# One tile shape for neighbouring matmuls in an attention and two-MLP kernel

## The chip, the cores and the metric

The kernel runs on one core of a Trainium2 chip. The metric is the device time of one execution in microseconds (us). Five engines work side by side and wait for each other through semaphores: TensorE (PE, with its weight loads listed as PEld), VectorE (DVE), ScalarE (ACT), GpSimd (POOL) and SyncE (SP), which issues the DMAs.

## The reference

The inputs are q, k, v of shape (4, 8, 576, 64) and a gate f of shape (4, 8, 576). In the computation below S = 576 and D = 64.

```python
scores = np.matmul(q, k.transpose(0, 1, 3, 2)) / np.sqrt(D)
cum = np.cumsum(np.log(np.clip(f, 0.0001, 1.0)), axis=-1)
decay = cum[:, :, :, None] - cum[:, :, None, :]
scores = np.where(causal, -1e9, scores + decay)      # causal: keys after the query
attn = np.exp(scores - scores.max(-1, keepdims=True))
attn = attn / (attn.sum(-1, keepdims=True) + 1e-9)
x = (attn @ v)                                       # then (2304 tokens, 512)
h = x @ w_in;   x = where(h >= 1, h, where(h <= -1, 0, (h + 1)**2 / 4)) @ w_out
h = x @ w_in2;  out = (P(h) / (Q(h) + 1e-6)) @ w_out2
```

P is a cubic in h with the four coefficients a, Q is 1 + |b0||h| + |b1|h². The weights are 512 x 2048 and 2048 x 512 and come as 64-bit floats.

## The kernel before

**Attention.** The 32 heads go in 16 pairs; the two heads of a pair lie in the lower and upper 64 partitions. For a pair, `tasks_of_pair` makes tasks for 9 blocks of queries. The first block holds the last 64 queries of both heads against all 576 keys (128-row matmuls, line 405). The other eight are four blocks of 128 queries for each of the two heads, against 512, 384, 256 and 128 keys. One task, S, computes such a block for both heads (line 414): four steps, each two matmuls side by side, one for each head in its own 64 partitions. The first three steps are the split products of q and k (each in a high and a low part, to keep fp32 accuracy): ql with kh, qh with kl, qh with kh. The fourth adds the decay of the keys: `one`, all ones, by `c_`, whose rows 0 and 1 (64 and 65 for the second head) hold the high and low part of the cumulated log of f; its other rows are zero. That step uses only 2 rows. M (VectorE) adds the causal mask and takes the maximum, E (ACT) the exp with its sum, T (line 460) transposes the block's exps in chunks of 128 keys into PSUM, C copies them to SBUF, and V (line 500) multiplies with v, chunk by chunk, for two groups of queries (256 and 320 wide), the two heads in two halves of the output's partitions. The fifth chunk has only 64 keys: its transpose has 64 columns, its product 64 rows. R1 to R6 divide: reciprocals of nine sums for each query (VectorE), a transpose of those 9 columns (line 528), a copy, a trip through memory that spreads them over partitions, and a product on POOL; X stores the pair's result.

**Filling work and MLPs.** During the attention, parts of the first MLP for early tokens fill the TensorE's free time (lines 683 and 764), and the 64-bit weights are turned into fp32 by steps on ACT and VectorE and split by ACT and POOL. Behind the attention both MLPs run over the rest (lines 683, 777, 779).

**The order.** It is written by `plan`, a list scheduler: each task has an engine, a duration, what it needs, and a key for its place; at each turn the task that can start first (with a small addition for its key) is taken, and buffers and queues are kept by the same durations. `plan` runs once for the attention with its filling work and once for the rest. Each engine then works off its own tasks in that order. So the durations given to S (line 424) and V (line 507) also set the order of all other tasks.

Of the kernel before, what the change touches and what calls it, by code (L numbers as in the profile page):

```python
# [7 lines left out]
F32 = mybir.dt.float32  # L8
# [4 lines left out]
ALU = mybir.AluOpType  # L13
# [5 lines left out]
def kernel(ctx, tc, qT, kT, v, f, w_in1, w_out1, w_in2, w_out2, a, b, out):  # L19
# [9 lines left out]
    P = 128  # L29
# [20 lines left out]
    CS = 12.0  # L50
    WARM, WARM2 = 12, 14
    WK = 0.003

    const = ctx.enter_context(tc.tile_pool(name="const", bufs=1))
    dram = ctx.enter_context(tc.tile_pool(name="dram", bufs=1, space=DRAM))
# [124 lines left out]
    kt, qt = [[[ap1.tile([P, S], F32R, name=f"{x}{y}{n}") for y in "hl"] for n in range(2)] for x in "kq"]  # L180
    qd = [[ap1.tile([P, P], F32R, name=f"qd{y}{n}") for y in "hl"] for n in range(2)]
    ct = [ap1.tile([P, S], F32R, name=f"ct{n}") for n in range(2)]
    one, oned = [ap1.tile([P, P], F32R, name=f"one{x}") for x in range(2)]
    half = ap1.tile([P, 2], F32, name="half")
    POOL.memset(half[:], 0.0)
# [16 lines left out]
    def load_pair(pr, x):  # L202
        if x < 2:
            t = ap2.tile([P, S], F32, tag=("ks", "qs")[x], name=f"{'kq'[x]}s{pr}")
            SP.dma_start(t[:], (kT, qT)[x][pr])
        else:
            t = ap2.tile([P, NC, P], F32, tag="vn", name=f"vn{pr}")
            SP.dma_start(
                t[:, 0:NC - 1, :], v[pr, 0:(NC - 1) * P, :].rearrange("(c p) d -> p c d", p=P)
            )  # L210
            SP.dma_start(t[0:QB, NC - 1, :], v[pr, (NC - 1) * P:S, :])
        nat[pr, x] = t

    def load_c(pr):
# [20 lines left out]
    def task(key, eng, dur, fn, deps=(), take=(), free=()):  # L235
# [2 lines left out]
        tasks.append((key, ways, tuple(d for d in deps if d is not None), tuple(take), tuple(free)))  # L238
        return len(tasks) - 1

    done, by = {}, {}
    clock = dict.fromkeys(LAT, T0)
    clock["sp"] = 3.0
    dma = [3.0, 5.0]
# [3 lines left out]
    def plan(first, wk):  # L248
        left, users = {}, {}
        for n in range(first, len(tasks)):  # L250
            users.setdefault(n, [])
            left[n] = 0
            for d in tasks[n][2]:
                if d >= first:
                    users.setdefault(d, []).append(n)
                    left[n] += 1
        ready = {n for n, k in left.items() if k == 0}
        order = []
        while ready:
            best = None  # L260
            for n in ready:
                key, ways, deps, take, _ = tasks[n]
                free_at = 0.0
                ok = True
                need = {}
                for tag in take:
                    k = need[tag] = need.get(tag, 0) + 1
                    if len(bufs[tag]) < k:
                        ok = False
                        break  # L270
                    free_at = max(free_at, sorted(bufs[tag])[k - 1])
                if not ok:
                    continue
                choice = None
                for w, (eng, dur, _) in enumerate(ways):
                    at = max(clock[eng], free_at)
                    for d in deps:
                        e2 = by[d]
                        at = max(at, done[d] + (0.13 if e2 == eng and eng != "pe" else 0.0 if e2 == eng else LAT[e2]))
                    end = at + dur if len(ways) > 1 else 0.0  # L280
                    if choice is None or end < choice[0]:
                        choice = (end, at, w)

                cand = (choice[1] + wk * key, key, n, choice[1], choice[2])
                if best is None or cand < best:
                    best = cand
            assert best, [(tasks[n][0], tasks[n][3]) for n in ready]
            _, key, n, at, w = best
            _, ways, _, take, free = tasks[n]
            eng, dur, fn = ways[w]  # L290
            ready.discard(n)
            by[n] = eng
            for tag in take:
                bufs[tag].remove(min(bufs[tag]))
            if eng == "sp":
                for issue, moved in dur:
                    dma[0] = max(dma[0], at) + issue
                    dma[1] = max(dma[1], dma[0] + 0.64) + MOVE * moved
                clock[eng] = dma[0]
                done[n] = dma[1] + LAND  # L300
            elif eng == "init":
                done[n] = dur
            else:
                clock[eng] = at + dur
                done[n] = at + dur
            for tag in free:
                bufs[tag].append(done[n] + LAT[eng])
            order.append((at, n, fn))
            for u in users[n]:
                left[u] -= 1  # L310
                if left[u] == 0:
                    ready.add(u)
        assert len(order) == len(left), (len(order), len(left))
        order.sort(key=lambda t: t[:2])
        return [t[1:] for t in order]

    def mm(n, passes=1):
        return passes * (max(n, 64) / 2400 + 0.013)
# [20 lines left out]
    def tasks_of_pair(pr):  # L339
# [48 lines left out]
        for pos, (b, j) in enumerate(BLOCKS):  # L388
# [8 lines left out]
            def s_fn(s=s, b=b, both=both, cuts=cuts):  # L397
# [12 lines left out]
                qc = slice(b * P, (b + 1) * P)  # L410
                for x, (qq, kk_) in enumerate(((ql_, kh), (qh, kl_), (qh, kh), (one, c_))):
                    for jj in range(2):
                        pp = slice(jj * QB, jj * QB + (QB if x < 3 else 2))
                        PE.matmul(  # L414
                            ts[jj][:, 0:n], qq[pp, qc] if x < 3 else qq[pp, :], kk_[pp, 0:n], start=(x == 0), stop=(x == 3)
                        )
# [3 lines left out]
            if j == 1:  # L420
                tid[pr, f"S{pos}"] = tid[pr, f"S{pos - 1}"]
            else:
                dur = 4 * sum(mm(n1 - n0) for n0, n1 in cuts) if both else 4 * max(mm(w), 0.22)
                T(f"S{pos}", s, "pe", 0.08 + dur, s_fn, ("klo", "ldc", "qlo", "qd0", "qd1", prev), ("S", "S"),
                  ("k", "q") if pos == NB - 2 else ())

            def max_fn(s=s, w=w, pos=pos, both=both):
                if pos == 0:
# [22 lines left out]

            firstg = pos == min(p for p, (bb_, _) in enumerate(BLOCKS) if int(bb_ * P >= GQ[0]) == g)
            for c0, c1 in [(0, LAST), (LAST, NC)] if both else [(0, b + 1)]:
                rows = QB if c0 == LAST else P

                def t_fn(s=s, c0=c0, c1=c1, rows=rows):
                    p = Pt[s]
                    ps = Tt[s, c0] = psT.tile([P, 512], F32, tag="T", name=f"T{s}_{c0}")
                    for c in range(c0, c1):
                        PE.transpose(  # L460
                            ps[0:rows, (c - c0) * P:(c - c0 + 1) * P], p[:, c * P:c * P + rows], ident[:]
                        )

                T(f"T{pos}_{c0}", s + KT, "pe", 0.107 * (c1 - c0), t_fn, (f"E{pos}",),
                  ("T",), ("P",) if c1 == b + 1 else ())

                def c_fn(eng, s=s, g=g, j=j, qo=qo, c0=c0, c1=c1, rows=rows, both=both):
                    if (pr, g) not in PT:
                        PT[pr, g] = ap1.tile([P, 2 + 3 * g, 2, GQ[g]], F32, tag=f"PT{g}", name=f"PT{pr}_{g}")
                    to, src = PT[pr, g], Tt.pop((s, c0))  # L470
                    n = (c1 - c0) * P
                    if both:
                        copy(eng, to[0:rows, c0:c1, :, qo:qo + QB], src[0:rows, 0:n].rearrange("p (c j x) -> p c j x", j=2, x=QB))
                    else:
                        copy(eng, to[0:rows, c0:c1, j, qo:qo + P], src[0:rows, 0:n].rearrange("p (c x) -> p c x", x=P))

                engs = ["act", "dve"]
                T(f"C{pos}_{c0}", s + KC, engs, [cost(e, (c1 - c0) * P, "ps") for e in engs],
# [5 lines left out]
        for g in (1, 0):  # L484
# [4 lines left out]
            deps = [k for k in list(tid) if k[0] == pr and k[1][0] == "C" and int(k[1][1:].split("_")[0]) in poss]  # L489
            for c in range(ncs):  # L490
                c_q = max(0, c * P - q0)
                rows = QB if c == LAST else P

                def pv_fn(g=g, c=c, c_q=c_q, rows=rows, n=n, ncs=ncs):
                    if c == 0:
                        Ot[pr, g] = psO.tile([P, 512], F32, tag="O", name=f"O{pr}_{g}")
                    o, pt = Ot[pr, g], PT[pr, g]
                    for j in range(2):
                        pp = slice(j * D, (j + 1) * D)
                        PE.matmul(  # L500
                            o[pp, c_q:n], nat[pr, 2][0:rows, c, pp], pt[0:rows, c, j, c_q:n],
                            start=(c == 0), stop=(c == ncs - 1),
                        )
                    if c == ncs - 1:
                        PT.pop((pr, g))

                T(f"V{g}{c}", s0 + last + KV, "pe", mm(n - c_q, 4) + 0.06, pv_fn,
                  deps + ["ldv"] + ([f"V{g}{c - 1}"] if c else []) + (["V14"] if g == 0 else []), ("O",) if c == 0 else (),
                  ((f"PT{g}",) + (("v",) if g == 0 else ())) if c == ncs - 1 else ())

            def o_fn(eng, g=g, q0=q0, n=n):
                if g == 1:
# [6 lines left out]


        def r1():
            r = Rt[pr] = ap2.tile([P, NB], F32, tag="r", name=f"r{pr}")
            DVE.tensor_scalar(out=r[:], in0=ls[pr][:], scalar1=1e-9, scalar2=None, op0=ALU.add)
            DVE.reciprocal(r[:], r[:])

        def r2():
            Rr[pr] = psT.tile([P, 512], F32, tag="T", name=f"rT{pr}")
            PE.transpose(Rr[pr][0:NB, 0:P], Rt[pr][:], ident[:])  # L528

        def r3():  # L530
            ps = Rr[pr]
# [560 lines left out]
```

## Time and profile before

| | |
|---|---|
| median of 3 runs | 1021.68 us (1020.82 to 1025.32) |
| the profiled execution | 1021.83 us, span 1020.0 us |
| mean granted TensorE clock | 0.990 |
| TensorE busy | 1003.8 us (98%), 5274 matmuls |
| weight loads busy | 796.4 us (78%) |
| VectorE busy | 739.6 us (73%) |
| ScalarE busy | 631.9 us (62%) |
| GpSimd busy | 377.0 us (37%) |

The span is the time from the first to the last instruction. TensorE's matmuls are pipelined and overlap in the trace, so that "busy" says little of how full it is; the distance from one start to the next is of more use. A line such as "64\*128 64x512" gives the rows and columns of the weights and the shape of the streamed operand. In the trace "L414" is line 414 of the kernel before.

### The profile page before, as it was taken

The page shows a single profiled execution, that of the slowest core. Times are in us where ns is not written, and L with a number is a line of the kernel's source. Part 1 is how long each engine was busy: PE and PEld are TensorE (multiplying, and loading weights), DVE is VectorE, ACT ScalarE, POOL GpSimd, SP SyncE. Part 2 cuts the span into 40 slices and gives each one's busy share as a digit, 9 for nine tenths or more (in the row PEclk, how much of TensorE's full clock was granted, in tenths as well). Part 3 has the DMA queues.
Part 4 walks back from the last instruction along what each step waited for, and adds up shares of the span by engine and source line. Part 5 has one row for each costly group of instructions (what it writes and reads, how often), then busy time and mean ns, then how long its engine had stood idle before and what let it go on. Part 6 is the DMA issues. An engine that isn't in the chain of part 4 may idle for free.

```text
span 1020.0 us, 15449 instructions
## 1 busy us (share of the span) xinstructions
PE 1003.8 (98%) x5274; PEld 796.4 (78%) x5274; DVE 739.6 (73%) x1411; ACT 631.9 (62%) x1312; POOL 377.0 (37%) x331
## 2 busy tenths in 40 slices
PE   8999999999999999999999999999999999999998
PEld 4665666666767888888888998888888888888887
DVE  6888997867287798786874577967667667657646
ACT  5787777767455443433432468876677667666666
POOL 3223320122365532222222133545454444445344
PEclk7999999999999999999999999999999999999999
DMA  5455766622456347565561454001101000010010
GB/s 187 152 176 172 220 204 204 190 67 69 158 189 227 118 152 238 161 205 166 156 225 63 131 179 125 1 10 33 42 0 42 8 35 16 6 42 1 1 42 21
DMA packets 62790, 113.13 MB, mean 111 GB/s; under 512 B 9452, under 2 KB 20348, under 8 KB 62712
## 3 DMA queue, kind: packets, MB, share of 16 engines
q1 hardware_dynamic: 62712, 112.15, 34.5%
q8 instruction: 42, 0.69, 0.3%
q14 instruction: 36, 0.29, 0.1%
HBM read 82.00 MB, written 30.11 MB: 110 GB/s over the span
## 4 chain that ended last, share of the span: by engine, by line
PE 89%; DVE 4%; ACT 2%; issue 2%; DMA 1%; POOL 1%; SPq 1%; ACTq 0%; DVEq 0%
PE h L683 35%; PE a L779 18%; PE a L777 16%; PE S L414 6%; PE T L460 5%; PE O L500 5%; PE a L764 2%; PE S L405 1%; DVE xl L672 1%; POOL wl L130 1%; ACT P L448 0%; DMA xr<-xd 0%; ACT PT L329 0%; DMA qs<-in_q_dram 0%; PE rT L528 0%
## 5 line engine op out<-in xcount | busy, mean ns | idle before, releaser
L697 POOL TENSOR_TENSOR gl<-t,gh 128x512 fp32r<-128x512 f32 (+1 forms) x160 | 195.7, 1224 | 323.3 <-ACT gh L693 238.9
L683 PE MATMUL h<-xl,wh 128*128 128x512 f32 (+1 forms) x640 | 236.5, 370 | 2.4 <-DVE xl L672 2.1
L683 PE MATMUL h<-xh,wl 128*128 128x512 f32 (+1 forms) x640 | 237.2, 371 | 1.0 <-ACT xh L668 1.0
L683 PE MATMUL h<-xh,wh 128*128 128x512 f32 (+1 forms) x640 | 235.6, 368 | 0.0
L693 ACT CAST gh<-t 128x512 fp32r<-128x512 f32 (+1 forms) x160 | 93.0, 582 | 112.7 <-PE a L779 47.8
L728 POOL TENSOR_TENSOR t<-t,t 128x512 f32<-128x512 f32 (+1 forms) x80 | 94.5, 1181 | 126.8 <-ACT t L721 123.4
L683 PEld LDWEIGHTS h<-xl,wh 128*128 128x128 f32 x640 | 120.7, 189 | 25.1 <-DVE xl L672 5.8
L683 PEld LDWEIGHTS h<-xh,wl 128*128 128x128 f32 x640 | 120.7, 189 | 22.3 <-ACT xh L668 1.4
L683 PEld LDWEIGHTS h<-xh,wh 128*128 128x128 f32 x640 | 120.7, 189 | 19.9
L779 PE MATMUL a<-wh,gl 128*128 128x512 f32 x288 | 112.3, 390 | 0.0
L779 PE MATMUL a<-wl,gh 128*128 128x512 f32 x288 | 112.2, 390 | 0.0
L779 PE MATMUL a<-wh,gh 128*128 128x512 f32 x288 | 112.1, 389 | 0.0
L777 PE MATMUL a<-gl,wh 128*128 128x512 f32 (+1 forms) x288 | 105.3, 366 | 0.0
L777 PE MATMUL a<-gh,wl 128*128 128x512 f32 (+1 forms) x288 | 105.3, 366 | 0.0
L777 PE MATMUL a<-gh,wh 128*128 128x512 f32 (+1 forms) x288 | 105.3, 365 | 0.0
L707 ACT ACTIVATE t<-t 128x512 f32<-128x512 f32 (+1 forms) x80 | 47.1, 589 | 91.6 <-DVE t L702 91.3
L746 DVE SCALAR_TENSOR_TENSOR t<-t,na,h 128x512 f32<-128x512 f32 (+1 forms) x80 | 55.4, 692 | 57.2 <-ACT h L742 56.1
L448 ACT ACTIVATE P<-P,nm 128x576 f32<-128x576 f32 (+2 forms) x144 | 83.7, 584 | 19.1 <-DVE nm L436 16.9
L702 DVE TENSOR_SCALAR t<-h 128x512 f32<-128x512 f32 (+1 forms) x80 | 50.7, 633 | 58.5 <-PE h L683 58.4
L732 DVE TENSOR_TENSOR t<-h,t 128x512 f32<-128x512 f32 (+1 forms) x80 | 51.0, 637 | 48.8 <-ACT t L724 48.5
L436 DVE CUSTOM_DVE_ANT_0 P<-S,tri 128x256 f32<-128x256 f32 (+1 forms) x144 | 66.9, 477 | 17.1 <-PE S L414 15.8
L718 ACT ACTIVATE t<-h,ab 128x512 f32<-128x512 f32 (+1 forms) x80 | 51.9, 651 | 41.9 <-PE h L683 41.7
(115 smaller groups left out, 1905.5 us busy)
## 6 DMA issues: line engine op xcount, KB each, us to landing
raw<-in_moe_w_in_dram SPq DMA_DIRECT2D x32, 512.0 KB
raw<-in_moe_w_out_dram SPq DMA_DIRECT2D x32, 512.0 KB
xr<-xd SPq DMA_DIRECT2D x48, 256.0 KB
wfd<-wd SPq DMA_DIRECT2D x44, 256.0 KB
wf<-wfd SPq DMA_DIRECT2D x44, 256.0 KB
ks<-in_k_dram SPq DMA_DIRECT2D x16, 288.0 KB
qs<-in_q_dram SPq DMA_DIRECT2D x16, 288.0 KB
xd<-xa SPq DMA_DIRECT2D x16, 288.0 KB
```

The lines of the kernel that those rows point to most:

```text
L414: PE.matmul(ts[jj][:, 0:n], qq[pp, qc] if x < 3 else qq[pp, :], kk_[pp, 0:n], start=(x == 0), stop=(x == 3))
L436: DVE.tensor_tensor_reduce(out=p[:, n0:n1], in0=t[:, 0:n1 - n0], in1=m, scale=-1.0 / ROOT, scalar=least, op0=ALU.add, op1=ALU.min, accum_o ...
L448: ACT.activation(p, p, AF.Exp, scale=-1.0, bias=nm[pr][:, pos:pos + 1], accum_out=ls[pr][:, COL[pos]:COL[pos] + 1])
L460: PE.transpose(ps[0:rows, (c - c0) * P:(c - c0 + 1) * P], p[:, c * P:c * P + rows], ident[:])
L683: PE.matmul(hps[g], ww[:, kk * P:(kk + 1) * P], xx[kk], start=(kk == 0 and y == 0), stop=(kk == KD - 1 and y == 2))
L693: ACT.copy(gt[g][0], mid[g][0])
L697: eng.tensor_tensor(out=lo, in0=mid.pop(g)[0], in1=hi.bitcast(F32), op=ALU.subtract)
L718: ACT.activation(mid[g]["w"], hps[g], AF.Abs, scale=ab[:, 0:1])
L728: POOL.tensor_tensor(out=vv, in0=vv, in1=mid[g]["w"], op=ALU.add)
L746: DVE.scalar_tensor_tensor(out=t, in0=t, scalar=na[:, 0:1], in1=hps[g], op0=ALU.add, op1=ALU.mult)
L777: PE.matmul(acc[x, d], ww[:, dd], gg, start=st, stop=sp)
L779: PE.matmul(acc[x, d], gg[:, dd], ww[:], start=st, stop=sp)
```

## The change

The fourth step of S takes all 64 rows of `one` and `c_` in place of 2. The last chunk of keys becomes 128 rows: its transpose takes the last 128 keys (448 to 575), and v's last chunk is loaded into partitions 64 to 127, with zeros below, so that the 64 keys that already were in the chunk before count nothing. For that, v and the reciprocals have two lasting tiles each, zeroed at the start; the transpose of the reciprocals covers all 128 columns. The planner has new durations for S and V, and a price for a change of shape (`SWC`, `SWT`) that is zero.

```diff
+    SWC, SWT = 0.0, 0.0
...
+    vt = [ap1.tile([P, NC, P], F32, name=f"vt{n}") for n in range(2)]
+
+    rt_ = [ap1.tile([P, P], F32, name=f"rt{n}") for n in range(2)]
+    for n in range(2):
+        POOL.memset(vt[n][0:QB, NC - 1, :], 0.0)
+        POOL.memset(rt_[n][:], 0.0)
...
-            t = ap2.tile([P, NC, P], F32, tag="vn", name=f"vn{pr}")
+            t = vt[pr % 2]
...
-            SP.dma_start(t[0:QB, NC - 1, :], v[pr, (NC - 1) * P:S, :])
+            SP.dma_start(t[QB:P, NC - 1, :], v[pr, (NC - 1) * P:S, :])
...
-                cand = (choice[1] + wk * key, key, n, choice[1], choice[2])
+                turn = SWC if ways[0][0] == "pe" and shape.get(n) != at_shape[0] else 0.0
+                cand = (choice[1] + turn + wk * key, key, n, choice[1], choice[2])
...
-                        pp = slice(jj * QB, jj * QB + (QB if x < 3 else 2))
+                        pp = slice(jj * QB, (jj + 1) * QB)
...
-                dur = 4 * sum(mm(n1 - n0) for n0, n1 in cuts) if both else 4 * max(mm(w), 0.22)
-                T(f"S{pos}", s, "pe", 0.08 + dur, s_fn, ("klo", "ldc", "qlo", "qd0", "qd1", prev), ("S", "S"),
+                dur = 4 * sum(mm(n1 - n0) for n0, n1 in cuts) if both else 4 * max(mm(w), 0.12)
+                T(f"S{pos}", s, "pe", 0.02 + dur, s_fn, ("klo", "ldc", "qlo", "qd0", "qd1", prev), ("S", "S"),
...
-                        PE.transpose(
-                            ps[0:rows, (c - c0) * P:(c - c0 + 1) * P], p[:, c * P:c * P + rows], ident[:]
-                        )
+                        k0 = min(c * P, S - P)
+                        PE.transpose(ps[:, (c - c0) * P:(c - c0 + 1) * P], p[:, k0:k0 + P], ident[:])
...
-                        copy(eng, to[0:rows, c0:c1, :, qo:qo + QB], src[0:rows, 0:n].rearrange("p (c j x) -> p c j x", j=2, x=QB))
+                        copy(eng, to[:, c0:c1, :, qo:qo + QB], src[:, 0:n].rearrange("p (c j x) -> p c j x", j=2, x=QB))
...
-                            o[pp, c_q:n], nat[pr, 2][0:rows, c, pp], pt[0:rows, c, j, c_q:n],
+                            o[pp, c_q:n], nat[pr, 2][:, c, pp], pt[:, c, j, c_q:n],
...
-                T(f"V{g}{c}", s0 + last + KV, "pe", mm(n - c_q, 4) + 0.06, pv_fn,
+                T(f"V{g}{c}", s0 + last + KV, "pe", mm(n - c_q, 4) + 0.03, pv_fn,
...
-            r = Rt[pr] = ap2.tile([P, NB], F32, tag="r", name=f"r{pr}")
+            r = rt_[pr % 2][:, 0:NB]
...
-            PE.transpose(Rr[pr][0:NB, 0:P], Rt[pr][:], ident[:])
+            PE.transpose(Rr[pr][:, 0:P], rt_[pr % 2][:], ident[:])
```

## Rows read from the trace of the kernel before

**Rows 1.** Busy time by stretch: PE, PEld, DVE, ACT, POOL, clock, DMA share, GB/s.

```profile
13.00:60.00 47.00, 46.06 (x303) 29.03 (x301) 37.48 (x123) 35.02 (x102) 11.84 (x11) 0.84 0.47 146
60.00:150.00 90.00, 86.26 (x598) 57.06 (x596) 83.97 (x222) 69.61 (x192) 27.54 (x23) 0.98 0.61 188
150.00:258.00 108.00, 108.00 (x762) 73.01 (x760) 79.29 (x235) 77.38 (x218) 18.32 (x17) 1.00 0.42 136
310.00:1000.00 690.00, 689.61 (x3290) 580.41 (x3289) 490.79 (x758) 405.71 (x718) 274.75 (x226) 1.00 0.28 89
```

**Rows 2.** Chain of waits by line, of 13:60, 60:150 and 150:258 us.

```profile
by line: PE S L414 33.0%; PE T L460 28.7%; PE O L500 24.2%; PE S L405 7.7%; SPq L211 2.7%; ACT PT L329 2.5%; PE rT L528 1.3%; ACT P L448 1.3%; SPq L208 0.8%; issue 0.6%; ACTq L329 0.1%
by line: PE S L414 17.4%; PE T L460 16.4%; PE O L500 13.8%; PE h L683 13.0%; ACT P L448 4.3%; issue 4.1%; PE S L405 3.5%; ACT PT L329 3.4%; DVE P L436 3.1%; PE a L764 3.1%; DVE kl L366 2.8%; DMA R<-rcd 2.5%; DVE xl L672 1.8%; DMA ct<-cd 1.5
by line: PE S L414 26.0%; PE T L460 22.6%; PE O L500 22.0%; PE a L764 11.8%; PE h L683 10.5%; PE S L405 6.0%; PE rT L528 1.4%
```

**Rows 3.** Windows of line 414 alone: PE, PEld, clock, DMA share, GB/s.

```profile
13.00:60.00 47.00, 17.70 (x110) 10.41 (x110) 0.84 0.47 146
60.00:150.00 90.00, 24.15 (x180) 14.35 (x178) 0.98 0.61 188
150.00:258.00 108.00, 29.99 (x224) 17.66 (x224) 1.00 0.42 136
```

**Rows 4.** Timeline of PE (start, length, instruction): a 512- and a 128-column group.

```profile
196.51 0.50 PE L414 MATMUL S<-kh,ql 64*128 64x512 f32 x2
196.84 0.39 PE L414 MATMUL S<-kl,qh 64*128 64x512 f32 x2
197.08 0.40 PE L414 MATMUL S<-kh,qh 64*128 64x512 f32 x2
197.40 0.49 PE L414 MATMUL S<-ct,one 2*128 2x512 f32 x2
197.83 0.28 PE L528 MATMUL rT<-ident,r 128*9 128x128 f32 x1
...
160.84 0.27 PE L414 MATMUL S<-kl,qh 64*128 64x128 f32 x2
160.95 0.27 PE L414 MATMUL S<-kh,qh 64*128 64x128 f32 x2
161.16 0.33 PE L414 MATMUL S<-ct,one 2*128 2x128 f32 x2
161.41 0.33 PE L460 MATMUL T<-ident,P 128*128 128x128 f32 x1
```

**Rows 5.** Weight loads by line and form: busy us, mean ns, idle before.

```profile
L460 PEld LDWEIGHTS T<-ident,P 128*128 128x128 f32 x384 | 44.4, 145 | 20.9 <-ACT P L448 8.9 <-issue 2.4 <-ACT PT L329 1.4
L414 PEld LDWEIGHTS S<-kl,qh 64*128 64x128 f32 x128 | 12.8, 197 | 0.0
L528 PEld LDWEIGHTS rT<-ident,r 128*9 128x9 f32 x16 | 1.4, 88 | 5.2 <-issue 3.6 <-DVE PT L331 0.7 <-PE S L414 0.4
```

**Rows 6.** Timeline of PE: the last chunk of keys in the product with v.

```profile
194.40 0.49 PE L500 MATMUL O<-PT,vn 128*64 128x192 f32 x3
194.81 0.33 PE L500 MATMUL O<-PT,vn 64*64 64x64 f32 x4
195.08 0.33 PE L460 MATMUL T<-ident,P 128*128 128x128 f32 x1
```

**Rows 7.** The start: a memset in POOL's timeline; TensorE's longest wait (us, times, longest).

```profile
2.87 0.45 POOL L186 MEMSET one<- 128x128 f32 x1
...
PE S L405 <- DMA ct<-ft: 2.9, 1, 2.9
```

**Rows 8.** Behind the attention: a piece of the chain in order, and TensorE's waits there.

```profile
257.97 7.71 PE a L764 x32
...
PE h L683 <- DVE xl L672: 2.1, 4, 1.1
```

**Rows 9.** Busy time by stretch again, ahead of and behind the clock's rise.

```profile
18.00:28.00 10.00, 9.61 (x42) 5.83 (x42) 6.69 (x23) 6.65 (x21) 1.40 (x2) 0.50 0.36 123
28.00:75.00 47.00, 45.48 (x350) 29.36 (x350) 41.89 (x134) 37.51 (x109) 13.00 (x11) 1.00 0.51 155
```

More of the change, by code (lines that the diff above doesn't have):

```diff
@@ L239, in task @@
         return len(tasks) - 1
+    shape = {}
     done, by = {}, {}
+    at_shape = [None]
     clock = dict.fromkeys(LAT, T0)
@@ L303, in plan @@
             else:
+                if eng == "pe" and shape.get(n) != at_shape[0]:
+                    at_shape[0] = shape.get(n)
+                    dur += SWT
                 clock[eng] = at + dur
@@ L422, in tasks_of_pair @@
             else:
-                dur = 4 * sum(mm(n1 - n0) for n0, n1 in cuts) if both else 4 * max(mm(w), 0.22)
-                T(f"S{pos}", s, "pe", 0.08 + dur, s_fn, ("klo", "ldc", "qlo", "qd0", "qd1", prev), ("S", "S"),
+                dur = 4 * sum(mm(n1 - n0) for n0, n1 in cuts) if both else 4 * max(mm(w), 0.12)
+                T(f"S{pos}", s, "pe", 0.02 + dur, s_fn, ("klo", "ldc", "qlo", "qd0", "qd1", prev), ("S", "S"),
                   ("k", "q") if pos == NB - 2 else ())
+                if not both:
+                    shape[tid[pr, f"S{pos}"]] = "rows"
             def max_fn(s=s, w=w, pos=pos, both=both):
@@ L453, in tasks_of_pair, with t_fn @@
             for c0, c1 in [(0, LAST), (LAST, NC)] if both else [(0, b + 1)]:
-                rows = QB if c0 == LAST else P
-                def t_fn(s=s, c0=c0, c1=c1, rows=rows):
+                def t_fn(s=s, c0=c0, c1=c1):
                     p = Pt[s]
@@ L459, in t_fn, with c_fn @@
                     for c in range(c0, c1):
-                        PE.transpose(
-                            ps[0:rows, (c - c0) * P:(c - c0 + 1) * P], p[:, c * P:c * P + rows], ident[:]
-                        )
+                        k0 = min(c * P, S - P)
+                        PE.transpose(ps[:, (c - c0) * P:(c - c0 + 1) * P], p[:, k0:k0 + P], ident[:])
                 T(f"T{pos}_{c0}", s + KT, "pe", 0.107 * (c1 - c0), t_fn, (f"E{pos}",),
                   ("T",), ("P",) if c1 == b + 1 else ())
-                def c_fn(eng, s=s, g=g, j=j, qo=qo, c0=c0, c1=c1, rows=rows, both=both):
+                def c_fn(eng, s=s, g=g, j=j, qo=qo, c0=c0, c1=c1, both=both):
                     if (pr, g) not in PT:
@@ L472, in c_fn @@
                     if both:
-                        copy(eng, to[0:rows, c0:c1, :, qo:qo + QB], src[0:rows, 0:n].rearrange("p (c j x) -> p c j x", j=2, x=QB))
+                        copy(eng, to[:, c0:c1, :, qo:qo + QB], src[:, 0:n].rearrange("p (c j x) -> p c j x", j=2, x=QB))
                     else:
-                        copy(eng, to[0:rows, c0:c1, j, qo:qo + P], src[0:rows, 0:n].rearrange("p (c x) -> p c x", x=P))
+                        copy(eng, to[:, c0:c1, j, qo:qo + P], src[:, 0:n].rearrange("p (c x) -> p c x", x=P))
                 engs = ["act", "dve"]
@@ L491, in tasks_of_pair, with pv_fn @@
                 c_q = max(0, c * P - q0)
-                rows = QB if c == LAST else P
-                def pv_fn(g=g, c=c, c_q=c_q, rows=rows, n=n, ncs=ncs):
+                def pv_fn(g=g, c=c, c_q=c_q, n=n, ncs=ncs):
                     if c == 0:
@@ L505, in pv_fn @@
                         PT.pop((pr, g))
-                T(f"V{g}{c}", s0 + last + KV, "pe", mm(n - c_q, 4) + 0.06, pv_fn,
+                T(f"V{g}{c}", s0 + last + KV, "pe", mm(n - c_q, 4) + 0.03, pv_fn,
                   deps + ["ldv"] + ([f"V{g}{c - 1}"] if c else []) + (["V14"] if g == 0 else []), ("O",) if c == 0 else (),
                   ((f"PT{g}",) + (("v",) if g == 0 else ())) if c == ncs - 1 else ())
+                shape[tid[pr, f"V{g}{c}"]] = "columns"
             def o_fn(eng, g=g, q0=q0, n=n):
@@ L521, in r1 @@
         def r1():
-            r = Rt[pr] = ap2.tile([P, NB], F32, tag="r", name=f"r{pr}")
-            DVE.tensor_scalar(out=r[:], in0=ls[pr][:], scalar1=1e-9, scalar2=None, op0=ALU.add)
-            DVE.reciprocal(r[:], r[:])
+            r = rt_[pr % 2][:, 0:NB]
+            DVE.tensor_scalar(out=r, in0=ls[pr][:], scalar1=1e-9, scalar2=None, op0=ALU.add)
+            DVE.reciprocal(r, r)
         def r2():
             Rr[pr] = psT.tile([P, 512], F32, tag="T", name=f"rT{pr}")
-            PE.transpose(Rr[pr][0:NB, 0:P], Rt[pr][:], ident[:])
+            PE.transpose(Rr[pr][:, 0:P], rt_[pr % 2][:], ident[:])
         def r3():
```

## The prediction

> **What bounds the kernel now.** The profiled execution spans 1020.0 us and took 1021.83 us as a run, 0.15 us above the median of the runs shown (1021.68), so the sum below is made against 1021.8 and needs no correction. I read the windows table first, cut into three attention stretches and the long stage behind them. From 310 to 1000 us TensorE is busy 689.6 of 690 us [rows 1]: nothing that the diff edits runs there, and whatever the attention gives back should arrive at the end unchanged. In the attention (13 to 258 us) TensorE is also busy nearly all the time, but so is VectorE in the middle: 84 of 90 us between 60 and 150, against 79 of 108 us behind it [rows 1]. A busy matmul row is no proof that the matmuls are late last, so I read the chain of waits for the same stretches next. From 13 to 60 us the matmul lines are 95% of it, from 60 to 150 us 67% (the rest is ACT's exps and copies, VectorE, DMA, issue), from 150 to 258 us all of it [rows 2]. A microsecond of TensorE time saved in these stretches is worth about those shares.
>
> How many saved steps lie in each stretch comes from the count of line 414's matmuls, eight to a group of scores: 110, 180 and 224 [rows 3], or 13.8, 22.5 and 28 groups. A pair of heads has four such groups, so this is 3.4, 5.6 and 7 of the 16 pairs.
>
> **The ones-by-c matmuls.** Starts in the timeline are the measure, because durations overlap. In the group of 512 columns, kl,qh to kh,qh takes 0.24 us from start to start: same 64-row shape, 512 columns at 2.4 GHz are 0.21 us, and the weights were loaded ahead. From kh,qh to ct,one, where the shape falls from 64 to 2 rows, it is 0.32, and from ct,one to the 128-row rT it is 0.43 [rows 4]. So a step into another shape costs 0.32 - 0.24 = 0.08 to 0.09 us more, and if the shape just entered lasts one step only, its exposed weight load adds another 0.43 - 0.32 = 0.11. The first step of the group shows the same: kh,ql to kl,qh is 0.33, also 0.1 over the 0.24 that follows it [rows 4]. The weight loads say it too: those of kl,qh have 0.0 us of idle time ahead of them [rows 5], they are loaded while the matmul before runs.
>
> With c on 64 rows, the three shapes 64, 2, 128 become 64, 128. The step into ct,one becomes a step inside a shape (0.24), the step out of it a plain change of shape (0.32): 0.56 in place of 0.75, a saving of 0.19. In the group of 128 columns the two steps are 0.21 and 0.25 [rows 4]; the step inside the shape is bound by the weight load at about 0.11 and the step out then 0.21, as the step out of kh,qh now: 0.32 in place of 0.46, a saving of 0.14. The groups of 384 and 256 columns show the pattern of the first (nothing in it depends on the columns as long as the weight load is hidden), so a pair saves 3 x 0.19 + 0.14 = 0.71 us, sixteen pairs 11.4 us. The rows of c that are added are zeros and stream in the same columns, so the matmuls themselves cost what they did.
>
> One rule speaks against this. The Trainium skill ("TensorE: Matmul & The Clock Gate", Part 3, What overlaps and what doesn't) says that a weight load overlaps a running matmul only where the row groups differ. By it the load for c, now in the rows where qh still streams, would be exposed. The row of kl,qh, in the same rows as the matmul ahead of it, with 0.0 us idle before its load, is against it [rows 5].
>
> **The last chunk of keys.** The product with v changes from 128x64 to 64x64 for one chunk of a pair: 194.40 to 194.81 into it, 194.81 to 195.08 until the next transpose starts [rows 6]. One change of shape goes (0.09), and with it the exposed load, here of 64 columns, about half of 0.1: 0.14 us a pair, between 0.05 (only the load) and 0.19 (a change with a full load). The streamed columns stay 64, so the 128 rows cost nothing more. Sixteen pairs: 2.2 us. The transposes of this chunk take 128 columns of weights in place of 64, the reciprocals 128 in place of 9. The mean loads are 145 ns for 128 columns and 88 ns for 9 [rows 5]; I charge 0.057 us for rT, and 0.03 for the chunk, since 64 columns lie halfway. I count no change of shape that goes away with these two, so they are losses: I take 0.07 us a pair, since some of the chunk's loads are hidden among other transposes; the bounds are 0 and 0.09.
>
> The Trainium skill (same page, LDWEIGHTS) prices a weight load by its columns at 1.2 GHz, which would make 9 to 128 columns 0.099 us dearer. The rows give 0.057; by the rule the whole gain would be 0.7 us smaller.
>
> **The rest of the diff.** Four more memsets on POOL stand ahead of those of ones and ct at the start. One of 128x128 took 0.45 us as the trace draws it; four are at most 1.8 us later on POOL, and TensorE waits 2.9 us there for the load of ct, behind VectorE's scan [rows 7]. That cover hides them; without it the price is 0 to 1.8 us. The two v loads go through SP as before, with the same bytes into other partitions and the same two buffers. The copies out of PSUM have twice the rows in the last chunk and the same columns; ACT has 30 us idle in the last stretch [rows 1], so even a dearer copy isn't on the path. The two switch prices in the planner are zero, so they do nothing; its prices for scores and v products fall, and with them the order of the attention can change. I cost this at nothing in the likeliest case, and come back to it.
>
> **The sum.** A pair saves 0.71 + 0.14 - 0.07 = 0.78 us of TensorE, 12.5 us in all. First stretch: 3.4 x 0.78 x 0.95 = 2.5. Middle: 5.6 x 0.78 = 4.4 to be had; the chain gives 67%, but VectorE at 93% takes some more, and I take half, 2.2 (bounds 0 and 4.4). Last: 7 x 0.78 = 5.5. Together 10.2 us: 1021.8 - 10.2 = 1011.6 us. What is late next is VectorE between 60 and 150 us, and TensorE still elsewhere.
>
> **Rivals.** *The gain is given back by order and cover.* The planner now prices the groups at 0.925, 0.712, 0.50 and 0.50 us (before 0.985 and 0.96 three times), 1.23 us a pair less, where I work out 0.71. VectorE's and ACT's queues keep their order, so each would stand up to 0.5 us a pair behind matmuls that were planned too early, 8 us in all. In the same way the last product of the filling work, 7.7 us of matmuls behind the last scores, covers the round trip of the last pair's reciprocals through memory; a planner that sees an emptier TensorE may run it earlier, and the 2.1 us of waiting for xl behind it would grow by up to 7.7 [rows 8]. Either gives 1014 to 1020 us. For it: the crowded middle. Against: in the last stretch TensorE is the whole chain, and there an early plan costs nothing.
>
> *The weights of c are not hidden.* Only the change of shape goes: 64 x 0.09 + 1.1 for v = 6.9 us of TensorE, and by the same shares (0.82 of it) 5.6 us: 1016.2 us. This is the rule above as a mechanism; the row speaks against it.
>
> *Slower: the clock.* From 18 to 28 us the granted clock is 0.50, that is 1.2 GHz, and 42 matmuls run in 10 us, against 350 in 47 us (74 in 10) right behind at 2.4 GHz [rows 9]. Ten microseconds more at the low level thus cost 10 x (1 - 42/74) = 4.3. If the shorter TensorE bursts leave more waiting in the crowded middle and the clock falls there as it did at the start after a wait, 24 us at the low level eat the 10.2, and 36 us more make it 1011.6 + 15.5 = 1027. For it: the mean of the middle is 0.98, so it fell there once too [rows 1]. Against: 1.00 all through the last stretch. The same mechanism can gain: an end of the low stretch before 28 us is worth up to 4.
>
> **Chances and range.** Forecast 0.70 (1006 to 1016.5), order and cover 0.19 (1014 to 1022), weights exposed 0.06 (1015 to 1018), clock 0.05 (1020 to 1035). Half a per cent, 5.1 us, is about what a measurement here can tell from no change, so faster is below 1016.6: 0.68 from the forecast, 0.07 and 0.03 from the second and third, 0.78. Same: 0.02 + 0.11 + 0.03 + 0.01 = 0.17. Slower: 0.01 + 0.04 = 0.05. The low end of the range, 1006, is all 12.5 us and an earlier end of the low clock; the high end, 1019, takes in most of the second case and all of the third.
>
> **What would show it.** In the changed profile ct,one has 64 rows; kh,qh to ct,one takes 0.23 to 0.24 us at 512 columns and ct,one to the next shape about 0.32; the 64x64 group of line 500 is gone, and the 0.41 us from the chunk before it to the last one falls by about 0.09; weight loads of rT rise from 88 to about 145 ns. The last scores' group starts about 10 us earlier, and the distance from there to the end is unchanged. The forecast is wrong if the steps shorten as said and the attention doesn't end 8 us or more earlier (VectorE or the order holds it), if it does and waits behind 258 us grow by as much, or if the step into ct,one stays above 0.3.

## The result and the profile after

The changed kernel takes 1008.45 us (median of 3 runs, 1006.85 to 1009.18) against 1021.68 us before: ratio 0.985, 95% interval 0.981 to 0.989. Five more runs on another occasion gave 1008.39 us and 0.987 (0.985 to 0.989). The forecast was 1011.6, range 1006 to 1019. The profiled execution took 1006.85 us with a span of 1004.8 us, at a mean TensorE clock of 0.999; the one before had 0.990.

The matmul steps come first, because the forecast hung on them. The timeline of PE in the changed kernel (start, length, instruction), for a group of 512 and one of 128 columns, to be read beside [rows 4]:

```profile
199.54 0.39 PE L430 MATMUL S<-kl,qh 64*128 64x512 f32 x2
199.77 0.39 PE L430 MATMUL S<-kh,qh 64*128 64x512 f32 x2
200.00 0.40 PE L430 MATMUL S<-ct,one 64*128 64x512 f32 x2
200.33 0.33 PE L544 MATMUL rT<-ident,rt 128*128 128x128 f32 x1
...
179.03 0.27 PE L430 MATMUL S<-kh,qh 64*128 64x128 f32 x2
179.14 0.28 PE L430 MATMUL S<-ct,one 64*128 64x128 f32 x2
179.34 0.33 PE L478 MATMUL T<-ident,P 128*128 128x128 f32 x1
```

Into ct,one it is now 0.23 us and out of it 0.33 (before 0.32 and 0.43); with 128 columns 0.11 and 0.20 (before 0.21 and 0.25). The predicted 0.56 and 0.32 for both steps together are measured as 0.56 and 0.31. The groups of 384 and 256 columns, which the forecast took to be like that of 512, fall from 0.63 to 0.44 and from 0.52 to 0.33 (medians of the groups at 2.4 GHz). The last chunk of keys in the product with v, beside [rows 6]:

```profile
185.29 0.49 PE L515 MATMUL O<-PT,vt 128*64 128x192 f32 x4
...
185.61 0.28 PE L515 MATMUL O<-PT,vt 128*64 128x64 f32 x4
185.83 0.33 PE L478 MATMUL T<-ident,P 128*128 128x128 f32 x1
```

From the chunk before to the last one 0.32 us in place of 0.41, from there to the transpose 0.22 in place of 0.27: 0.14 us less, as worked out. The weight loads by form (busy us, mean ns, idle ahead), beside [rows 5]; the first line is that of the kernel before:

```profile
L414 PEld LDWEIGHTS S<-ct,one 2*128 2x128 f32 x128 | 12.2, 188 | 13.9 <-issue 10.7
...
L430 PEld LDWEIGHTS S<-ct,one 64*128 64x128 f32 x128 | 12.4, 185 | 0.7
L430 PEld LDWEIGHTS S<-kl,qh 64*128 64x128 f32 x128 | 12.3, 186 | 0.0
L544 PEld LDWEIGHTS rT<-ident,rt 128*128 128x128 f32 x16 | 2.2, 139 | 5.7 <-issue 2.2 <-ACT PT L345 1.5 <-DVE nm L454 0.7
```

The loads of c had 13.9 us of idle time ahead of all 128 of them before, and have 0.7 now: they are hidden, as those of kl,qh are. The load for the reciprocals went from 88 to 139 ns.

Where the time went by stretch: windows of the changed kernel, with the columns of [rows 1].

```profile
13.00:60.00 47.00, 42.35 (x336) 28.60 (x333) 43.84 (x133) 39.97 (x113) 13.89 (x12) 1.00 0.55 166
60.00:150.00 90.00, 87.02 (x627) 60.24 (x626) 84.79 (x228) 71.81 (x199) 23.98 (x22) 1.00 0.61 194
150.00:258.00 108.00, 107.85 (x764) 78.60 (x763) 75.62 (x224) 73.99 (x208) 24.34 (x22) 1.00 0.45 149
310.00:1000.00 690.00, 689.62 (x3307) 581.04 (x3306) 488.74 (x766) 406.06 (x727) 275.67 (x231) 1.00 0.27 84
```

The first stretch gets through more work than before (336 matmuls in 47 us against 303) with TensorE busy for less of it, at a clock of 1.00 where it had 0.84, and VectorE is now at 43.8 of 47 us where it was at 37.5. The chain of waits for 60 to 150 us, beside the second line of [rows 2]:

```profile
by line: PE T L478 16.1%; PE S L430 14.4%; PE O L515 13.8%; PE h L699 12.9%; PE a L780 7.9%; DVE P L454 6.4%; PE S L421 5.0%; DVE kl L382 3.5%; ACT P L466 3.3%; DMA R<-rcd 3.2%; DVE ql L382 2.9%; DVE rt L539 2.6%; DVE PT L347 2.1%; issue 1.
```

Line 454, VectorE's maximum, has doubled there, from 3.1 to 6.4%. Behind the attention nothing moved: the last filling product, a piece of the chain in order, and TensorE's waits from 235 to 310 us, beside [rows 8].

```profile
242.61 7.66 PE a L780 x32
```

```profile
PE h L699 <- DVE xl L688: 2.2, 4, 1.1
PE h L699 <- ACT xh L684: 1.0, 1, 1.0
```

It starts 257.97 - 242.61 = 15.4 us earlier, and the span is 15.2 us shorter. The cover of 7.7 us and the waiting for xl (2.1 us before, 2.2 now) are as they were, and so is the 1.0 us for xh. All of the gain was made in the attention. One part of it isn't in the matmul steps, as the windows ahead of and behind 28 us show, beside [rows 9]:

```profile
18.00:28.00 10.00, 9.09 (x65) 5.49 (x61) 9.80 (x30) 7.68 (x23) 2.09 (x3) 1.00 0.40 135
28.00:75.00 47.00, 43.44 (x348) 29.51 (x347) 43.75 (x140) 41.71 (x118) 13.96 (x12) 1.00 0.55 163
```

The clock stood at 0.50 from 18 to 28 us before, and at 1.00 in this execution; 65 matmuls ran there in place of 42. That is partly chance: the changed kernel too can have a low stretch there, as the profile of e6 below shows.

### The profile page after: what moved, and what is told of

The parts are those of the page before. It is cut to its first block, busy times and chain, and to the rows that moved or that the text cites. A ratio compares the mean times of both kernels' runs of the same rounds, so it can differ in the third digit from the quotient of the medians.

```text
span 1004.8 us, 15464 instructions
## 1 busy us (share of the span) xinstructions
PE 986.7 (98%) x5274; PEld 792.3 (79%) x5274; DVE 740.6 (74%) x1412; ACT 630.6 (63%) x1310; POOL 379.3 (38%) x336
## 4 chain that ended last, share of the span: by engine, by line
PE 87%; DVE 7%; issue 2%; ACT 2%; POOL 1%; DMA 1%; SPq 1%; DVEq 0%; POOLq 0%; ACTq 0%
PE h L699 36%; PE a L795 19%; PE a L793 16%; PE O L515 4%; PE T L478 4%; PE S L430 4%; PE a L780 2%; PE S L421 1%; DVE xl L688 1%; DVE P L454 1%; POOL wl L131 1%; DVE wd L97 1%; ACT P L466 1%; DVE wd L101 0%; DVE wd L107 0%
## 5 line engine op out<-in xcount | busy, mean ns | idle before, releaser
L478 PE MATMUL T<-ident,P 128*128 128x128 f32 x400 | 68.7, 284 | 7.1 <-ACT P L466 2.9
```

The lines of the kernel that those rows point to most:

```text
L478: PE.transpose(ps[:, (c - c0) * P:(c - c0 + 1) * P], p[:, k0:k0 + P], ident[:])
```

## The experiments

Three theories stood against each other: the shapes (steps on TensorE), the new order of the planner, and the clock at the start. Each kernel ran several times beside the kernel before; the table gives the median time, the median of the runs' mean clocks, and the ratio of the times to before on the same chip (worked out over all runs, so that it isn't quite that of the medians).

| kernel | us | clock | ratio, 95% interval |
|---|---|---|---|
| before (74 runs, four occasions) | 1021.2, 1020.9, 1022.0, 1020.8 | 0.991 | |
| e0 changed kernel | 1008.39 | 0.996 | 0.987 (0.985 to 0.989) |
| e1 before, c on 64 rows | 1010.60 | 0.997 | 0.988 (0.985 to 0.990) |
| e2 before, new durations | 1024.21 | 0.990 | 1.001 (1.000 to 1.003) |
| e3 changed, old durations | 1008.58 | 0.997 | 0.987 (0.984 to 0.989) |
| e4 before, longer warm-up | 1019.22 | 0.994 | 0.997 (0.995 to 1.000) |
| e5 changed, longer warm-up | 1009.07 | 0.996 | 0.988 (0.985 to 0.990) |
| e6 changed, reciprocals on 9 columns | 1008.35 | 0.996 | 0.987 (0.985 to 0.990) |
| e7 changed, c on 2 rows | 1023.83 | 0.988 | 1.002 (1.000 to 1.004) |
| e8 before, c on 32 rows | 1020.90 | 0.991 | 0.998 (0.996 to 1.000) |
| e9 before, c on 33 rows | 1009.28 | 0.998 | 0.986 (0.984 to 0.989) |
| e10 changed, shorter warm-up | 1008.68 | 0.998 | 0.986 (0.983 to 0.989) |
| e11 changed, a price for shape changes | 1020.08 | 0.990 | 0.999 (0.998 to 1.001) |

**e0, the changed kernel again.**

> The changed kernel again, beside the others on one chip. All theories: about 13 us faster than before (1008.5 against 1021.7, ratio 0.987). If a low TensorE clock at the start belongs to the kernel before and not to chance, its mean clock stays near 0.99 in every run of before and near 0.997 here.

Measured 1008.39 us, clocks 0.994 to 0.998. The runs of before in the four sets had 0.984 to 0.993, and never more. So the higher clock goes with the changed kernel, though how much of it a single execution gets is chance.

**e1, c on 64 rows alone**, in the order of before on every engine.

```diff
-                        pp = slice(jj * QB, jj * QB + (QB if x < 3 else 2))
+                        pp = slice(jj * QB, (jj + 1) * QB)
```

> Kernel before with the ones-by-c product on 64 rows and nothing else; durations in the planner as before, so every engine's order is that of before. Shapes theory: 11.4 us of TensorE go, times the chain's share of 0.82 about 9.3 us: 1012 us. Order theory (the new durations give the gain): 1021 to 1022. Clock theory (the low stretch at the start is what went): 1021.7 when the clock is low from 11 to 28 us, some 7 us less when it isn't, whatever the shapes.

1010.60 us: 10.6 of the 12.8 us, with this one line.

**e2, the order alone**, with the old shapes.

```diff
-                dur = ... else 4 * max(mm(w), 0.22)
-                T(f"S{pos}", s, "pe", 0.08 + dur, ...
+                dur = ... else 4 * max(mm(w), 0.12)
+                T(f"S{pos}", s, "pe", 0.02 + dur, ...
...
-                T(f"V{g}{c}", ..., mm(n - c_q, 4) + 0.06, ...
+                T(f"V{g}{c}", ..., mm(n - c_q, 4) + 0.03, ...
```

> Kernel before with the three new durations in the planner (0.12 and 0.02 for S, 0.03 for V) and the old shapes. Shapes theory: 1020 to 1024, the order is worth nothing by itself. Order theory: 1013 or less.

1024.21 us, nothing gained; the ratio's interval reaches from no change to 0.3% slower, or 3 us.

**e3, the shapes in the old order**: the same three numbers put back in the changed kernel.

> Changed kernel with the three old durations in the planner: all new shapes in the old order. Shapes theory: 1009 to 1012, within 3 us of the changed kernel. Order theory: 1018 or more.

1008.58 us, the changed kernel's time. With e2 this settles the order as a source of the gain: it gave nothing, and with the new shapes it took nothing that these runs can tell.

**e4, a longer warm-up before.**

```diff
-    task(-99, "pe", 0.22 * WARM2, lambda: warm(WARM2), (t,), ("T",), ("T",))
+    task(-99, "pe", 0.22 * WARM2, lambda: warm(22), (t,), ("T",), ("T",))
```

> Kernel before with 22 warm-up matmuls in place of 14 in the second warm-up group (the planner's duration for it unchanged, so the order is as before): TensorE has less idle time ahead of the first product with c. Clock theory: the low clock from 11 to 28 us goes in most runs, and with it up to 17 x 0.43 = 7 us: 1015 to 1018. Rival (the stretch to 28 us is held by ACT, VectorE and DMA as well, or the clock falls anyway): 1020 to 1023.

1019.22 us, between the two expectations, and it spread: 1015.5 to 1025.2 us at clocks from 0.999 down to 0.987. The clock differs by chance here, and the time goes with it. Over 81 runs of before (without the set beside e11, which would move the line by 0.1 us), e4 and e8, which have the same steps and the same order, a straight line through time and clock falls by 0.75 us for each 0.001 of clock and stands at 1018.3 us for 0.995. Over the 22 runs of the changed kernel, e5, e6 and e10 it stands at 1009.3 for 0.995. At this clock the two differ by 9.0 us. The lines aren't parallel (0.75 and 0.37 us for each 0.001): the difference falls from 9.8 us at 0.993 to 7.9 at 0.998, so that 9.0 is good to about 1 us. The rest of the 12.8 us goes with the clock that each usually gets (0.991 and 0.996).

e4 and e3 also serve to check the stretches: both work off the old order, and TensorE started these instructions of line 405 (421 in the changed kernel) and the last of line 528 (544) at

| first scores of pair (counted from 0) | 0 | 4 | 9 | last transpose of reciprocals |
|---|---|---|---|---|
| e4, old shapes (us) | 10.2 | 61.7 | 143.5 | 251.7 |
| e3, new shapes (us) | 9.4 | 58.4 | 139.8 | 243.2 |
| stretch, e4 less e3 | | 2.5 | 0.4 | 4.7 |

The longer warm-up puts off e4's first scores by 0.8 us, but the first product with c, for which both wait, by only 0.4 (12.2 and 11.8 us); counted from there the first stretch is 3.0. From 60 to 150 us the clocks differed, in the windows of e3 and then of e4:

```profile
60.00:150.00 90.00, 85.51 (x612) 58.87 (x611) 84.94 (x226) 70.05 (x193) 28.93 (x23) 0.98 0.66 207
```

```profile
60.00:150.00 90.00, 86.60 (x601) 57.51 (x601) 84.63 (x227) 71.00 (x197) 28.14 (x23) 1.00 0.63 202
```

A mean of 0.98 is 3.6 of the 90 us at half speed. What such a microsecond costs follows from the two lines: 0.001 of the mean clock is 2.0 us at half speed in a span of 1018 us, so by estimate it is 0.37 us with the slope of before and 0.18 with that of the changed kernel, less than the 0.43 of the forecast. That makes 0.6 to 1.3 us, and at one clock the middle is worth 1.0 to 1.7.

**e5, the same warm-up in the changed kernel.**

> Changed kernel with the same 22 warm-up matmuls. If the profiled run of the changed kernel (clock 0.999) had luck that its other runs (0.996) had not: 1006 to 1007 in all runs. Rival: 1008.5 as the changed kernel, or up to 1.7 us slower because the first scores start later.

1009.07 us, clocks 0.996 to 1.000: no gain. The rival holds, and the 0.999 of the first profiled execution was luck.

**e6, the reciprocals on 9 columns.**

```diff
-            PE.transpose(Rr[pr][:, 0:P], rt_[pr % 2][:], ident[:])
+            PE.transpose(Rr[pr][0:NB, 0:P], rt_[pr % 2][:, 0:NB], ident[:])
```

> Changed kernel with the reciprocals' transpose back on 9 columns of weights. My price (0.057 us a pair dearer with 128): 0.9 us faster than the changed kernel, near 1007.6. Rival (9 columns are a shape of their own and cost a change): slower by 16 x 0.09 to 0.19, 1.4 to 3 us.

1008.35 us: neither the 0.9 us that I priced nor the rival's 1.4 to 3 show in the time, whose interval is 5 us wide. The timelines show the step from rT to the v product, of e6 and then of the changed kernel:

```profile
161.96 0.28 PE L544 MATMUL rT<-ident,rt 128*9 128x128 f32 x1
162.16 0.65 PE L515 MATMUL O<-PT,vt 128*64 128x256 f32 x4
```

```profile
229.16 0.33 PE L544 MATMUL rT<-ident,rt 128*128 128x128 f32 x1
229.42 0.87 PE L515 MATMUL O<-PT,vt 128*64 128x256 f32 x8
```

0.20 us with 9 columns and 0.26 with 128. So 128 columns cost 0.05 to 0.06 us there, and 9 columns were no shape of their own: from rT to a transpose of 128 columns it takes 0.12 us with 9 columns, and 0.11 between two transposes of 128. This part of the change is a small loss on TensorE that no run could tell from nothing.

The profile of e6 also has a long low stretch. Its window from 18 to 28 us:

```profile
18.00:28.00 10.00, 9.76 (x44) 5.54 (x42) 7.29 (x22) 6.26 (x17) 0.86 (x3) 0.53 0.26 80
```

At a clock of 0.53 the new shapes get 44 matmuls through, hardly more than the 42 of before. So the 65 of the first execution follow from its clock rather than explain it.

**e7, c back on 2 rows in the changed kernel** (the edit of e1 the other way round).

> Changed kernel with the ones-by-c product back on 2 rows, all else changed (order, v, reciprocals). Shapes theory: the 9 to 11 us of this part come back: 1018 to 1020. If the order or the v chunk carried most of the gain: 1012 or less.

1023.83 us: 15.4 us are lost, more than expected, at a median clock of 0.988. With e1 it shows that most of the gain hangs on this line. That it lost more than e1 gained is the clock in part (0.996 to 0.988, by e4's line an estimated 6 us); what the rest of the change gives lies between 0.4 us (e2 to e7) and 2 us (e1 to e3) and isn't measured closer.

**e8 and e9, 32 and 33 rows** in the kernel before.

```diff
-                        pp = slice(jj * QB, jj * QB + (QB if x < 3 else 2))
+                        pp = slice(jj * QB, jj * QB + (QB if x < 3 else 32))
```

> Kernel before with 32 rows in the ones-by-c product in place of 2, order as before. Theory (what costs is the change between the 64-row and a smaller tile shape, and up to 32 rows are the smaller one): nothing changes, 1020 to 1022, steps of 0.32 and 0.43 us into and out of it at 512 columns, mean clock near 0.99. Rival (the number of rows that work sets the step or the clock): part of the way towards 1010.

> The same with 33 rows, one more. Theory (33 rows need the 64-row shape): as with 64 rows, 1008.5 to 1012.7, steps of 0.23 and 0.32 us, mean clock 0.993 to 0.998. Rival (a shape is left only by exactly the same number of rows): 1020 to 1022. Rival for the clock (few active rows keep it low): steps as with 64 rows, but a clock near 0.99 and 1013 or more.

1020.90 and 1009.28 us: one row more takes off 11.6 us. The timelines of e8 and then of e9:

```profile
195.63 0.40 PE L414 MATMUL S<-kh,qh 64*128 64x512 f32 x2
195.96 0.49 PE L414 MATMUL S<-ct,one 32*128 32x512 f32 x2
196.38 0.28 PE L528 MATMUL rT<-ident,r 128*9 128x128 f32 x1
```

```profile
199.63 0.39 PE L414 MATMUL S<-kh,qh 64*128 64x512 f32 x2
199.85 0.39 PE L414 MATMUL S<-ct,one 33*128 33x512 f32 x2
200.18 0.28 PE L528 MATMUL rT<-ident,r 128*9 128x128 f32 x1
```

0.33 and 0.42 us with 32 rows, as with 2; 0.22 and 0.33 with 33, as with 64. The clock goes the same way. The windows from 18 to 28 us of e8 and of e9:

```profile
18.00:28.00 10.00, 9.61 (x42) 5.73 (x42) 7.27 (x25) 6.92 (x22) 1.35 (x2) 0.55 0.33 119
```

```profile
18.00:28.00 10.00, 8.89 (x63) 5.54 (x64) 9.53 (x29) 8.79 (x29) 2.97 (x3) 1.00 0.44 146
```

0.55 with 32 rows and 1.00 with 33; the runs' clocks are 0.989 to 0.993 and 0.997 to 0.998. So it isn't the number of rows at work that goes with the clock (33 rows and the 64 of e1 have 0.998 and 0.997); in this order the higher clock came with the shorter steps.

**e10, a shorter warm-up in the changed kernel** (4 in place of 14 in e4's line).

> Changed kernel with 4 warm-up matmuls in the second group in place of 14, so that TensorE idles some 2 us longer ahead of the first product with c; the planner's duration is unchanged, and so is the order. If that wait makes the clock fall: a low stretch from about 11 us in every run, mean clock 0.992 or less, 1011 to 1014. If the changed kernel's denser matmuls bring the clock back soon in any case: 1008 to 1010, mean clock 0.995 or more.

1008.68 us at clocks of 0.996 to 0.998, although TensorE's wait for ct is now 4.2 us (2.2 in e0's profile, 2.9 in [rows 7]). The wait and two windows of e10:

```profile
PE S L421 <- DMA ct<-ft: 4.2, 1, 4.2
...
8.00:18.00 10.00, 5.47 (x29) 4.13 (x29) 5.61 (x14) 3.76 (x8) 0.97 (x1) 0.83 0.71 231
18.00:28.00 10.00, 8.75 (x63) 5.64 (x64) 9.87 (x28) 8.39 (x26) 2.83 (x4) 1.00 0.39 121
```

By these mean clocks it was low for some 3.4 us; before, with the shorter wait, it was still at 0.50 from 18 to 28 us. A longer wait ahead of c did not bring a longer low stretch.

**e11, a price for a change of shape.** Since a change costs up to 0.2 us with its load and 214 are left in the attention, I tried the planner's own switch.

```diff
-    SWC, SWT = 0.0, 0.0
+    SWC, SWT = 0.1, 0.2
```

> Changed kernel with prices for a change of shape in the planner: 0.1 us when it chooses the next task, 0.2 us of TensorE time. In TensorE's order 129 changes of shape are left of 214 in the attention. If each still costs 0.09 + 0.1 us and TensorE is the bound: 85 x 0.19 = 16 us of TensorE, with the chain's share of 0.82 13 us, near 995 us. Rival (matmuls of one shape are now waited for, and the waits of scores, exps and transposes take the place of the changes): 1003 to 1015, with more of TensorE's idle time behind ACT and VectorE.

1020.08 us: 85 changes fewer, and 11.7 us lost. The window from 60 to 150 us, TensorE's waits from 13 to 250 us and the chain of that window:

```profile
60.00:150.00 90.00, 82.88 (x596) 61.78 (x596) 79.95 (x209) 68.56 (x189) 25.95 (x23) 0.98 0.64 205
```

```profile
PE T L478 <- ACT P L466: 3.2, 6, 1.0
PE T L478 <- ACT rr L549: 3.2, 4, 1.2
PE S L430 <- DVE nm L454: 3.1, 6, 2.0
```

```profile
by line: PE O L515 8.0%; issue 7.2%; DVE P L454 6.8%; DMA raw<-in_moe_w_out_dram 6.2%; PE a L780 6.2%; PE h L699 6.1%; PE T L478 5.9%; PE S L430 5.7%; ACT P L466 5.7%; DMA raw<-in_moe_w_in_dram 3.7%; DMA R<-rcd 3.0%; ACT PT L345 2.9%; DVE w
```

596 matmuls get through where the changed kernel does 627, and TensorE's lines are a third of the chain in place of two thirds. Scores now wait for the maximum of others (3.1 us), transposes for the copy of the reciprocals (3.2). The rival had it, even beyond its 1015. The last transpose of the reciprocals starts at 251.8 us here, 8.9 later than in e0's profile, so most of the loss arises in the attention. The clock went down as well, to a median of 0.988; in the profile the longest low stretch lies behind the attention, where the longest wait for xh has grown from 1.0 to 4.4 us:

```profile
PE h L699 <- ACT xh L684: 5.4, 3, 4.4
...
280.00:293.00 13.00, 7.32 (x17) 4.90 (x17) 10.38 (x14) 4.91 (x9) 6.78 (x5) 0.50 0.54 185
```

So fewer changes of shape do not hold the clock up by themselves.

## Why the prediction was right, and where it was off

**The steps.** All three prices were right to 0.01 us: 0.19 and 0.14 for c (measured 0.19 and 0.15), 0.14 for the last chunk, and a loss of 0.05 to 0.06 for rT where it follows a change of shape. The rival by which c's weights would stay exposed is refuted by the 0.7 us of idle time ahead of 128 loads.

**The place.** 2.5, 2.2 and 5.5 us were forecast for the three stretches, 10.2 together. e4 against e3 gives 2.5 to 3.0, 1.0 to 1.7 (with the clock's estimate) and 4.7, together 8.2 to 9.4; at one clock the runs give 9.0. So the steps were worth about 1 us less than forecast. Of the 4.4 us to be had in the crowded middle more than half was given back; the half in the sum was a guess. That VectorE takes it is suggested by the doubled share of line 454 in the chain, and not tested. Why the last stretch gave 4.7 of 5.5 stays open.

**The distance behind the attention** did not change, and the order gained nothing, so the first rival had no part in it.

**The clock is the term that was mis-sized.** I costed it at nothing in the likeliest case, and put it among the rivals as a risk, for shorter bursts of TensorE would leave more waiting; its gain side, "worth up to 4", only widened the range. The runs show that it gained: the median clock rose from 0.991 to 0.996, which is 3.4 us on top of 9.0 by the two lines of e4 (0.75 us for each 0.001 before, 0.37 after). Its sign was wrong in the argument: with the new shapes in this order the clock is usually low for less time and not for more. Its price, 0.43 us for each microsecond at the low level, was too high as well (0.18 to 0.37 by the lines). The forecast of 1011.6 is thus off by two errors of opposite sign, about 1 us too much for the steps and 3.4 too little for the clock; the rest of its 3.2 us is of the size of the scatter of the runs around the lines, 0.7 us. Why the clock comes back sooner stays open: that it isn't the rows at work (e8, e9) nor the wait for c alone (e10) is shown, and e11 shows that fewer changes of shape aren't enough.

## What to carry to other kernels

In the timeline, compare the distance from start to start of equal matmuls with that across a change of tile shape; here such a change cost 0.09 us, and 0.1 more where the next load could not run ahead. Zero rows that keep neighbours in one shape cost nothing here where the columns stayed the same, so try padding ahead of reordering: with this planner and the two prices of e11, gathering equal shapes by the order cost more in waits than it saved. And when two kernels run at different mean clocks, fit time against clock over many runs before crediting the whole difference to the edit.

## What the runs showed of the hardware that was not expected

Between 32 and 33 rows the step into and out of the product with c changes from 0.33 and 0.42 us to 0.22 and 0.33, with nothing between: 33 rows step as 64 do, and 32 as 2. The transpose with 9 columns of weights among those with 128 is no such change. And the mean clock of one and the same kernel differs from run to run (0.984 to 0.993 before), and with it the time, by up to 8 us within one set (1018.1 to 1026.5 beside e4).
